# Strided sparse attention feeding a bilinear layer: later batches' attention at other places of the matmul stream, more seven-product pairs, and strided values loaded densely and spread by ScalarE

## The chip, the cores and the metric

The kernel runs on one core of a Trainium2 chip. Its engines work from queues of their own: TensorE (PE, with its weight loads listed as PEld), VectorE (DVE), ScalarE (ACT), GpSimd (POOL) and SyncE (SP); POOL and SP issue nearly all the DMAs. The metric is the device time of one execution in microseconds, lower is better.

## The reference

```python
# q, k, v: (8 batches, 8 heads, 576 positions, 64); scale = 1 / 8
rel = pos[:, None] - pos[None, :]
mask_local = (rel >= 0) & (rel < 32)                       # heads 0 to 3
mask_strided = (rel >= 0) & (pos[None, :] % 32 == pos[:, None] % 32)   # heads 4 to 7
attn = softmax(where(mask, scale * q @ k.T, -1e9))
x = (attn @ v), tokens by heads: 4608 x 512
out = ((x @ w_a) * (x @ w_b)) @ w_out                      # d_ff = 1536
```

## The kernel before

**The bilinear layer sets the pace.** The 4608 tokens are cut into nine tiles t of 512. A tile has 16 slots: twelve feature slots (`ffn_ab`, one block of 128 of the 1536 features each: products with w_a and w_b, 512 columns wide and four deep) and four output slots (`ffn_y` or `ffn_ys`). In this text a slot number counts within its tile, 0 to 11 for features and 12 to 15 for the output stage; tile t's slot s is number 16t + s in the code. An ordinary feature slot puts w_a's product and w_b's product into two PSUM banks; ACT copies the first to `a_sb` (L638) and DVE multiplies the two into `pf` (L641).

**Seven-product pairs.** For some pairs g of feature blocks (2g, 2g+1) the product with w_a is formed from seven half-size products in place of eight (`a_pair_mid` for tiles 3 to 6, listed in `MID_A`; `a_pair` for tiles 7 and 8, listed in `FAST_A`): 14 matmuls of 256 columns in place of 8 of 512. The pair needs four differences of the x tile (`xsum_make`, DVE, L672) and one more bank X: the bank named `e` in `a_pair_mid`. A pair fills slots 2g and 2g+1. From tile 1 on the output stage is done with seven products too (`y_plan`): 14 groups of six matmuls of 256 columns in the order `Y_ORDER`; "yN" is the point just after the Nth group, so y4 lies in slot 13, y7 at its end, y12 in slot 15. It uses sums of `pf` that DVE forms beforehand (`fast_s`, L820); ACT (L851, L857) and DVE (L849, L853, L855) empty its banks.

**Attention is threaded into that stream.** Each later batch b is cut into eight units u, 0 to 3 for the local heads and 4 to 7 for the strided ones. Its steps are:

- D: DMA transposes on SP (`step_D`) that bring k to `kT` and q to `qT`; the rows come from a cast load to DRAM on POOL (`load_qk`);
- Q0 to Q3 (`step_Q`, L338): DVE copies qT into the zero-padded `qz`; Q0 and Q1 are the two halves of the local heads, Q2 and Q3 of the strided heads;
- Su: score matmuls (L381) from `kT` and both halves of `qz` into the one `st` buffer, exp on ACT (L401), mask on DVE (L419);
- Vu for u 0 to 3 (`step_V`): p times `vl` into PSUM bank `o` (L462), then reciprocal (L470) and product (L488) on DVE into `xl`;
- Vu for u 4 to 7 (`step_VT`): p times `vs` into the banks `o` and `e` (L521), Ln twice (L533), Exp (L534) on ACT, two products on DVE (L536) into `xT`;
- O0, O1 (`rows_out`) and I0, I1 (`rows_in`): the local heads' rows go to DRAM and come back transposed into `xT`, both on SP.

The PSUM banks from tile 3 on are three `mm`, one `tp`, the two of `st`, one `o` and one `e`; before tile 3 there is no `e`, and `o` is one buffer of two banks. A buffer that is single is free again when its last reader has ended.

**The order is written out by hand.** `STEPS` (batches 1, 2), `LATER` and `IN_Y` (batches 3 to 7) give for each step the slot after which it is issued; `run` issues all of a step's instructions, on every engine, at that point, and the code keeps each engine's instructions in that order. In `LATER` a number x means slot 16(b-1) + x, so -4 is slot 12 of tile b-2 and 0 is slot 0 of tile b-1; `IN_Y` gives places yN in the output stage of tile b-1. Loads, D, `wsum_make`, `xsum_make` and `fast_s` are placed by `do(slot, ...)`; within a slot the matmuls come first, then the steps of the tables, then the `do` entries. From slot 14 on POOL's work of a slot waits behind a small copy into `pace` of what the slot made.

Of the kernel before, what the change touches and what calls it, by code (L numbers as in the profile page):

```python
# [8 lines left out]
BF16 = mybir.dt.bfloat16  # L9
# [5 lines left out]
FIRST_D = 2  # L15
RL = 6
RS = 8
NP = 72
# [6 lines left out]
VW = 128  # L25
WCH = (0, 2, 5, 9, 12)
FAST_Y = (1, 2, 3, 4, 5, 6, 7, 8)
MID_A = {t: (1, 3) for t in (3, 4, 5, 6)}
FAST_A = {7: (1, 2, 3, 4, 5), 8: (0, 1, 2, 3, 4, 5)}


@with_exitstack
def kernel(
# [10 lines left out]
    nc = tc.nc  # L44
# [23 lines left out]
    def open_psum(stack, **bufs):  # L68
        for nm, n in bufs.items():
# [12 lines left out]
    qT = (const.tile([128, 2, S], BF16, name="qTl"), const.tile([128, HL * W], BF16, name="qTs"))  # L82
    kT_buf = [(const.tile([128, 2, PAD + S], BF16, name=f"kT{i}l"), const.tile([128, 2, RS * GP + 48], BF16, name=f"kT{i}s"))
              for i in range(2)]
    vl_buf = [const.tile([128, HL * 6, VW], BF16, name=f"vl{i}") for i in range(2)]

    p_buf = [const.tile([128, 2, PW], BF16, name=f"p{i}") for i in range(5)]
    vs_buf = [const.tile([NP, HL, RS, VW], BF16, name=f"vs{i}") for i in range(2)]
    mask_l = const.tile([128, 4, LW], I16)
    mask_s = const.tile([NP, NP], I16)  # L90
    nm_l = const.tile([128, 128], BF16, name="nml")
# [139 lines left out]
    def load_vs(b, heads=range(HL)):  # L231
        if b < FIRST_D:

            for z in range(2):
                t = blocks("k", z)
                nc.gpsimd.dma_start(out=t[:NP, :, :RS * D],
                                    in_=v[b, HL + 2 * z:HL + 2 * z + 2].rearrange("h (p r) d -> p h (r d)", r=RS))
                nats[b, "v", z] = t
            return
        for h in heads:  # L240
            nc.gpsimd.dma_start(out=vs_buf[b % 2][:, h, :, 0:D],  # L241
                                in_=v[b, HL + h].rearrange("(p r) d -> p r d", r=RS))

    def spread_vs(b, h, eng):
        eng(vs_buf[b % 2][:, h, :, 0:D], nats[b, "v", h // 2][:NP, h % 2, :RS * D].rearrange("p (r d) -> p r d", r=RS))

    def load_w(c):
        f = slice(128 * WCH[c], 128 * WCH[c + 1])
# [85 lines left out]
    def step_Q(b, z, j):  # L334

        r = slice(64 * j, 64 * j + 64)
        dst = qz_buf[b % 2][j][z][r]
        nc.vector.tensor_copy(dst.rearrange("d c r n -> d (c r n)") if z else dst, qT[z][r])  # L338
# [220 lines left out]
    def step_X(b, c):  # L559
# [15 lines left out]
    STEPS = {1: {5.5: "Tk2", 6: "Tq2", 7: "S4 Tk3", 7.5: "S5", 8: "Tq3", 8.5: "V4", 9: "S6 V5 Pk0", 9.5: "S7 Pq0",  # L575
                 10: "V6 Tk0", 10.5: "Tq0 Pk1", 11: "Pq1", 12: "V7 Tk1 S0 W0 W1", 12.5: "Tq1 W2",
                 12.6: "S1", 12.75: "L0 X2", 13: "s2 X3 V0 m2 L1 W3", 13.5: "V1 S3", 14: "V2 X0", 14.5: "V3", 15: "X1"},
             2: {18: "Q0 Q1", 20: "S0", 20.5: "S1", 21: "V0", 21.5: "S2 Q2", 22: "V1 Q3", 22.5: "S3 O0", 23: "V2", 23.5: "S4",
                 24: "V3 I0 O1", 24.5: "S5", 25.5: "V4", 26: "S6", 26.5: "I1", 27: "V5", 27.5: "S7", 28.5: "V6", 30: "V7"}}
    LATER = {-4: "Q0", -3: "Q1", -1: "S0", 0: "S1", 1: "V0", 2: "S2 Q2", 3: "V1 O0", 4: "S3 I0 Q3", 5: "V2", 6: "S4", 7: "V3 O1", 8: "S5", 9: "V4 I1",  # L580
             10: "S6",
             11: "V5"}
    IN_Y = {2: "S7", 6: "V6", 11: "V7"}
    FN = {"Tk": step_Tk, "Tq": step_Tq, "S": step_S, "V": step_V, "X": step_X, "W": lambda b, n: fast_w(n, slice(0, 3)),
          "s": S_px, "m": S_m, "L": lead_vl, "O": rows_out, "I": rows_in, "Pk": lambda b, c: pair_up("k", c), "Pq": lambda b, c: pair_up("q", c),
          "Q": lambda b, n: step_Q(b, n // 2, n % 2)}

    def run(b, slot):
        for s in slot:
# [13 lines left out]
    def mm_bank(shape):  # L603
        nm = "tp" if used[0] % 4 == 3 and used[0] >= 0 else "mm"
        used[0] += 1
        return psum4[nm].tile(shape, F32, tag=nm, name="mm")
# [61 lines left out]
    def xsum_make(t, n):  # L668
        s_ = xsum[t]
        a, b = ((x_part(t, 0, 1), x_part(t, 0, 0)), (x_part(t, 1, 1), s_[:, 0]), (x_part(t, 1, 1), x_part(t, 0, 1)),  # L670
                (x_part(t, 1, 0), s_[:, 1]))[n]
        nc.vector.tensor_tensor(s_[:, n], a, b, op=ALU.subtract)  # L672
# [3 lines left out]
    def a_pair_mid(t, g):  # L676

        pf = pfs[t]
        X = psum4["e"].tile([128, 512], F32, tag="e", name="e")[:, :HT]
        Y, Z, b1, b0 = [mm_bank([128, TTOK]) for _ in range(4)]  # L680
        Y, Z = Y[:, :HT], Z[:, :HT]
        a = [fsb.tile([128, TTOK], F32, tag="a_sb", name="a_sb", bufs=3) for _ in range(2)][::-1]
        p7 = fsb.tile([128, HT], F32, tag="p7", name="p7")
        quarter = lambda e, k: a[e][:, HT * k:HT * (k + 1)]

        def P(bank, lhs, rhs, start=False):
            for c in range(2):
                nc.tensor.matmul(bank, lhsT=lhs(c), rhs=rhs(c), start=start and c == 0, stop=c == 1, skip_group_check=True)

        w = lambda e, j: (lambda c: wav[:, j, c, g, e])  # L690
        ws = lambda n: (lambda c: wsum_a[n][:, c, g])
        x = lambda j, k: (lambda c: x_part(t, j, k)[:, c])
        xs = lambda n: (lambda c: xsum[t][:, n, c])

        def b_mm(bank, e, kks):
            f = 2 * g + e
            x0 = TTOK * t % (XR * S)
            for kk in kks:
                for k in range(2) if x0 + TTOK > XR * S else (None,):
                    rhs = x_part(t, kk // 2, k)[:, kk % 2] if k is not None else xT[:, kk, x0:x0 + TTOK]  # L700
                    dst = bank if k is None else bank[:, HT * k:HT * (k + 1)]
                    nc.tensor.matmul(dst, lhsT=wb_sb[:, kk, 128 * f:128 * (f + 1)], rhs=rhs,  # L702
                                     start=kk == 0 and k in (None, 0), stop=kk == KD - 1 and k in (None, 1))

        def mult(e, bank):
            halves = lambda v_: v_.rearrange("p (a i s) -> p a i s", i=2, s=16)
            nc.vector.tensor_mul(pf[:, 2 * g + e, :].rearrange("p (i a s) -> p a i s", i=2, s=16), halves(a[e]), halves(bank))

        def add(q, other):
            nc.vector.tensor_tensor(q, other, q, op=ALU.add)  # L710

        P(Y, w(0, 1), x(1, 0), True)
        P(X, w(0, 0), x(0, 0), True)
        nc.scalar.copy(quarter(0, 0), X)
        b_mm(b1, 1, (0, 1, 2))
        P(X, ws(1), xs(1))
        nc.scalar.copy(quarter(1, 0), X)
        P(Z, ws(2), xs(2), True)
        nc.scalar.copy(p7, Z)
        b_mm(b1, 1, (3,))  # L720
        add(quarter(0, 0), Y)
        yield p7[:1, :1]
        P(X, ws(0), xs(0))
        nc.scalar.copy(quarter(1, 1), X)
        b_mm(b0, 0, (0,))
        P(Z, w(1, 1), xs(3))
        add(quarter(1, 0), Z)
        add(quarter(1, 1), p7)
        b_mm(b0, 0, (1, 2, 3))
        P(X, ws(3), x(1, 1))  # L730
        nc.scalar.copy(quarter(0, 1), X)
        mult(1, b1)
        mult(0, b0)
        yield pf[:1, 2 * g, :1]
# [242 lines left out]
    with tc.manual_schedule(engines={ENG.PE, ENG.SP, ENG.Pool, ENG.DVE, ENG.Activation}):  # L977
# [76 lines left out]
        for t in range(NT):  # L1054
            slots += [(ffn_ab, t, f) for f in range(FD)] + [(ffn_ys if t in FAST_Y else ffn_y, t, j) for j in range(4)]
        for b in range(1, B):
            for pos, names in (STEPS.get(b) or {16 * (b - 1) + x: n for x, n in LATER.items()}).items():
                steps.setdefault(pos, []).append((b, names.split()))
            if b not in STEPS:
                for n, names in IN_Y.items():  # L1060
                    steps["y", b - 1, n] = [(b, names.split())]

        at = {}

        def do(i, fn, *args):
            at.setdefault(i, []).append(lambda: fn(*args))
# [10 lines left out]
        for b in range(FIRST_D, B):  # L1077
            g0 = 16 * (b - 2)
            if b == FIRST_D:
                do(0, load_qk, b, False)  # L1080
                do(1, load_qk, b, True)
                do(14, load_vl, b)
                for h in range(HL):
                    do((16, 18, 19, 20)[h], load_vs, b, (h,))
            else:
                do(19 if b == FIRST_D + 1 else g0 - 2, load_qk, b, False)
                do(21 if b == FIRST_D + 1 else g0 + 2, load_qk, b, True)
                for h in range(HL):
                    do(g0 + h + (15 if b == FIRST_D + 1 else 10), load_vs, b, (h,))
                do(g0 + (12 if b == FIRST_D + 1 else 7), load_vl, b)  # L1090
            gs = {2: (13, 14, 15, 15), 3: (6, 6, 14, 15)}.get(b) or (3, 4, 10, 11)
            for (z, nm), g in zip(((0, "k"), (0, "q"), (1, "k"), (1, "q")), gs):
                do(g0 + g, step_D, b, z, nm)
        for n in range(4):
            for c in range(2):
                do(16 * 2 + (2, 5, 7, 9, 11, 13, 14, 15)[2 * n + c], wsum_make, n, c)
        for t in MID_A:
            do(16 * t - 1, xsum_make, t, 0)
            for n in (1, 2, 3):
                do(16 * t, xsum_make, t, n)  # L1100
        do(16 * (NT - 2) - 1, xsum_make, NT - 2, 0)
        for n in (2, 1, 3):
            do(16 * (NT - 2), xsum_make, NT - 2, n)
        for n in range(4):
            do(16 * (NT - 2) + 12 + n, xsum_make, NT - 1, n)
        for h in range(HL):
# [61 lines left out]
```

## Time and profile before

| | before |
|---|---|
| runs, us | 323.25, 323.65, 330.45; median 323.65 |
| profiled execution, us | 323.88, of which the profiled span is 322.2 |
| busy us | PE 313.8, DVE 248.4, ACT 191.4, POOL 120.2 |
| DMA | 40.41 MB in 127811 packets |
| `vs` loads on POOL | 24 of 72 KB, 905 ns each to issue, 4.9 us to landing (median) |
| feature slots of tiles 3, 4, 5 begin at | 126.8, 160.2, 193.7 us |
| output stages of tiles 2, 3, 4, 5 begin at | 116.6, 150.0, 183.5, 216.8 us |

The page gives busy time and counts for each engine. In the order of time, each line has a start, a duration, engine, line, operation, what it writes and reads, the form, how many instructions are merged, and in square brackets the engine's idle time before it and what ended it. Ends of matmuls are modelled, so their durations overlap; their starts are measured. A few per cent of the matmul records are missing.

### The profile page before, as it was taken

What the parts mean: (1) busy time and instruction counts of PE and PEld (TensorE: products, weight loads), DVE (VectorE), ACT (ScalarE), POOL (GpSimd) and SP (SyncE); (2) the same over time, 40 slices, a digit from 0 to 9 for tenths busy, and PEclk for the clock granted to TensorE, in tenths of its full rate; (3) what the DMA queues carried; (4) which work ended last, traced back from release to release, by engine and by line L of the source; (5) the groups of instructions that cost most, each with busy time, mean ns of one, the idle gap of its engine ahead of it and who ended that gap; (6) DMA issues with size and microseconds to landing.
All of it is one profiled execution on the core that took longest, in us unless ns stands there. A gap on an engine that the chain in (4) does not pass through costs nothing. (4 is left out here: it accounts for less than half of the span.)

```text
span 322.2 us, 7287 instructions
## 1 busy us (share of the span) xinstructions
PE 313.8 (97%) x2738; PEld 217.9 (68%) x2766; DVE 248.4 (77%) x569; ACT 191.4 (59%) x371; POOL 120.2 (37%) x211
## 2 busy tenths in 40 slices
PE   8999999999999999999999999999999999999994
PEld 7764555455775578556999996559655866786684
DVE  6665797488867988899689868997799667857862
ACT  6763767355854476557655766577656655535541
POOL 8844850881255344315340435134001003203520
PEclk9999999999999999999999999999999999999999
DMA  8999999999599999999997999999235040004004
GB/s 154 146 203 199 203 190 209 174 146 152 119 126 144 209 148 104 144 157 172 123 120 151 164 108 131 158 203 135 18 85 121 2 127 5 0 4 130 3 0 130
DMA packets 127811, 40.41 MB, mean 125 GB/s; under 512 B 115616, under 2 KB 124896, under 8 KB 127584
## 3 DMA queue, kind: packets, MB, share of 16 engines
q0 software_dynamic: 80400, 19.28, 65.3%
q1 hardware_dynamic: 47232, 20.61, 35.9%
q8 instruction: 21, 0.34, 0.5%
q14 instruction: 14, 0.11, 0.1%
q10 hardware_dynamic: 144, 0.07, 0.1%
HBM read 39.12 MB, written 18.28 MB: 178 GB/s over the span
## 5 line engine op out<-in xcount | busy, mean ns | idle before, releaser
L617 PE MATMUL mm<-xT,wb_sb 128*128 128x512 bf16 (+1 forms) x301 | 71.6, 357 | 0.4
L617 PE MATMUL mm<-xT,wa_sb 128*128 128x512 bf16 (+1 forms) x287 | 70.2, 356 | 0.6
L638 ACT COPY a_sb<-mm 128x512 f32<-128x512 f32 x68 | 39.7, 584 | 29.5 <-PE mm L617 27.8
L1134 POOL CAST pace<-pf 1x1 f32<-1x1 bf16 x68 | 18.5, 273 | 87.6 <-DVE pf L641 41.0
L617 PEld LDWEIGHTS <-wb_sb 128*128 128x128 bf16 x312 | 30.0, 98 | 27.8 <-issue 0.7
L641 DVE TENSOR_TENSOR pf<-a_sb,mm 128x512 bf16<-128x512 f32 x58 | 39.4, 680 | 9.4 <-ACT a_sb L638 5.7
L401 ACT ACTIVATE p<-st 72x576 bf16<-72x576 f32 (+1 forms) x56 | 36.4, 650 | 15.4 <-PE st L381 14.7
L617 PEld LDWEIGHTS <-wa_sb 128*128 128x128 bf16 x312 | 27.9, 98 | 17.8
L886 PEld LDWEIGHTS <-ps 128*128 128x128 bf16 x336 | 32.6, 98 | 4.1 <-issue 0.5
L886 PE MATMUL mm<-wf,ps 128*128 128x256 bf16 x252 | 30.0, 273 | 0.3 <-ACT y_sb L851 0.3
L851 ACT COPY y_sb<-mm 128x512 f32<-128x512 f32 (+1 forms) x32 | 17.9, 558 | 19.1 <-PE mm L886 16.4
L1134 POOL COPY pace<-y_sb 1x1 f32<-1x1 f32 x21 | 8.4, 401 | 51.2 <-DVE y_sb L849 23.6
L886 PEld LDWEIGHTS <-pf 128*128 128x128 bf16 x252 | 23.6, 98 | 2.7
L766 PE MATMUL mm<-xT,wb_sb 128*128 128x512 bf16 x83 | 25.3, 379 | 0.1
L241 POOL DMA_DIRECT2D vs<-in_v_dram x24 | 21.7, 905 | 4.1 <-issue 1.7
L886 PE MATMUL mm<-wo_sb,pf 128*128 128x256 bf16 x168 | 21.8, 273 | 0.0
L820 DVE TENSOR_TENSOR ps<-pf 128x512 bf16<-128x512 bf16 (+1 forms) x49 | 19.6, 399 | 0.8
L702 PE MATMUL mm<-xT,wb_sb 128*128 128x512 bf16 (+1 forms) x80 | 19.1, 337 | 0.0
L419 DVE TENSOR_TENSOR p<-p,mask_l 128x576 int16<-128x576 int16 x32 | 14.5, 452 | 5.6 <-ACT p L401 5.5
L536 DVE TENSOR_TENSOR xT<-o,xr 64x288 bf16<-64x288 f32 x16 | 7.6, 477 | 13.5 <-ACT xr L534 13.4
L462 PEld LDWEIGHTS <-p 128*128 128x128 bf16 (+1 forms) x256 | 12.9, 97 | 7.1 <-DVE xl L488 1.1
L488 DVE TENSOR_TENSOR xl<-o,rc 96x384 bf16<-96x384 f32 x24 | 13.3, 553 | 0.8
(212 smaller groups left out, 644.0 us busy)
## 6 DMA issues: line engine op xcount, KB each, us to landing
out_dram<-y_sb SPq DMA_DIRECT2D x14, 512.0 KB, 4.6
kr<-in_k_dram POOLq DMA_DIRECT2D x12, 288.0 KB, 6.2
qr<-in_q_dram POOLq DMA_DIRECT2D x12, 288.0 KB, 7.1
vl<-in_v_dram POOLq DMA_DIRECT2D x6, 384.0 KB, 9.3
out_dram<-y_sb SPq DMA_DIRECT2D x7, 256.0 KB, 5.5
vs<-in_v_dram POOLq DMA_DIRECT2D x24, 72.0 KB, 4.9
xd<-xl SPq DMA_DIRECT2D x12, 144.0 KB, 3.3
wo_sb<-in_moe_w_out_dram POOLq DMA_DIRECT2D x4, 384.0 KB, 10.7
```

Source lines behind the costliest of these rows:

```text
L241: nc.gpsimd.dma_start(out=vs_buf[b % 2][:, h, :, 0:D], in_=v[b, HL + h].rearrange("(p r) d -> p r d", r=RS))
L401: nc.scalar.activation(p_flat(p)[:M, :2 * W].rearrange("p (i n) -> p i n", n=2 * n), st[:M].rearrange("p a (i n) -> p (a i) n", n=256)[:, ...
L419: nc.vector.tensor_tensor(pi, pi, mk, op=ALU.bitwise_and)
L617: nc.tensor.matmul(ps_[:, c0:c0 + n], lhsT=w[:, kk, 128 * f:128 * (f + 1)], rhs=xT[:, kk, x0:x0 + n], start=(kk == first and c0 == 0), sto ...
L638: nc.scalar.copy(a_sb, ab[0])
L641: nc.vector.tensor_mul(pf[:, f, :].rearrange("p (i a s) -> p a i s", i=2, s=16), halves(a_sb), halves(ab[1]))
L702: nc.tensor.matmul(dst, lhsT=wb_sb[:, kk, 128 * f:128 * (f + 1)], rhs=rhs, start=kk == 0 and k in (None, 0), stop=kk == KD - 1 and k in (N ...
L766: nc.tensor.matmul(got[e], lhsT=wb_sb[:, kk, 128 * f:128 * (f + 1)], rhs=xT[:, kk, x0:x0 + TTOK], start=kk == 0, stop=kk == KD - 1)
L820: nc.vector.tensor_tensor(s[:, n], a, b, op=op)
L851: nc.scalar.copy({"1": part(0, 0), "7": part(0, 1), "6": part(1, 0), "5": part(1, 1)}[k], bank)
L886: nc.tensor.matmul(bank[b][:, q], lhsT=lhs(g, q), rhs=rhs(g), start=k in "172" and q == 0 and g == 0, stop=g == FG - 1, skip_group_check=True)
L1134: nc.gpsimd.tensor_copy(pace, done)
```

## The change

- `LATER` is replaced for batches 4 to 7 and now also holds places in output stages: ("y", N) with positive N is yN of tile b-1, with negative N it is y(14+N) of tile b-2. S0 goes from slot 15 of tile b-2 to y4 of that tile, S1 from slot 0 to y7, S4 from slot 6 to y12, V0 from slot 1 to y13; Q0 and Q1 from slots 12 and 13 to 11 and 12, Q2 and Q3 from slots 2 and 4 of the next tile to 13; in tile b-1, V1 goes from slot 3 to 1, V4 from 9 to 2, V2 from 5 to 3, V3 from 7 to 5, V5 from 11 to 6, V6 from y6 to 10, V7 from y11 to y2. Batch 3 keeps the old places (`THIRD`).
- More seven-product pairs, also at g = 0; there two of the pair's banks are exchanged, and one matmul pair of w_b is issued earlier in every mid pair. The four x differences of tiles 4 to 7 are made at y7 and y9 of the tile before.
- The strided values of a batch come by one load into `v_rows`, and ScalarE copies each head into `vs` (R0 to R3). `vl` rows become 66 elements wide in place of 128. Loads and the transposes of the strided heads are issued some slots sooner.

```diff
-MID_A = {t: (1, 3) for t in (3, 4, 5, 6)}
-FAST_A = {7: (1, 2, 3, 4, 5), 8: (0, 1, 2, 3, 4, 5)}
+MID_A = {3: (2, 4), 4: (0, 2, 4), 5: (0, 2, 4), 6: (0, 2, 4)}
+FAST_A = {7: (0, 1, 2, 3, 4, 5), 8: (0, 1, 2, 3, 4, 5)}
...
-    vl_buf = [const.tile([128, HL * 6, VW], BF16, name=f"vl{i}") for i in range(2)]
+    vl_buf = [const.tile([128, HL * 6, D + 2], BF16, name=f"vl{i}") for i in range(2)]
+    v_rows = const.tile([NP, HL, RS * D], BF16, name="v_rows")
...
-        for h in heads:
-            nc.gpsimd.dma_start(out=vs_buf[b % 2][:, h, :, 0:D],
-                                in_=v[b, HL + h].rearrange("(p r) d -> p r d", r=RS))
+        nc.gpsimd.dma_start(out=v_rows, in_=v[b, HL:].rearrange("h (p r) d -> p h (r d)", r=RS))
...
-        eng(vs_buf[b % 2][:, h, :, 0:D], nats[b, "v", h // 2][:NP, h % 2, :RS * D].rearrange("p (r d) -> p r d", r=RS))
+        src = v_rows[:, h] if b >= FIRST_D else nats[b, "v", h // 2][:NP, h % 2, :RS * D]
+        eng(vs_buf[b % 2][:, h, :, 0:D], src.rearrange("p (r d) -> p r d", r=RS))
...
-    LATER = {-4: "Q0", -3: "Q1", -1: "S0", 0: "S1", 1: "V0", 2: "S2 Q2", 3: "V1 O0", 4: "S3 I0 Q3", 5: "V2", 6: "S4", 7: "V3 O1", 8: "S5", 9: "V4 I1",
-             10: "S6",
-             11: "V5"}
-    IN_Y = {2: "S7", 6: "V6", 11: "V7"}
+    THIRD = {-4: "Q0", -3: "Q1", -1: "S0 R0", 0: "S1", 1: "V0 R1", 2: "S2 Q2", 3: "V1 O0 R2 R3", 4: "S3 I0 Q3", 5: "V2", 6: "S4", 7: "V3 O1", 8: "S5",
+             9: "V4 I1", 10: "S6", 11: "V5", ("y", 2): "S7", ("y", 6): "V6", ("y", 11): "V7"}
+    LATER = {-8: "R0", -7: "R1", -5: "Q0 R2", -4: "Q1 R3", ("y", -10): "S0", ("y", -7): "S1", -3: "Q2 Q3", ("y", -2): "S4", ("y", -1): "V0",
+             0: "S2", 1: "V1 O0", 2: "V4 S3", 3: "V2 S5 I0", 5: "V3 O1", 6: "V5 S6", 7: "I1", 9: "S7", 10: "V6",
+             ("y", 2): "V7", ("y", 7): "x0 x1", ("y", 9): "x2 x3"}
...
+        if g == 0:
+            Z, b1 = b1, Z
...
+        b_mm(b0, 0, (0,))
         P(X, ws(0), xs(0))
         nc.scalar.copy(quarter(1, 1), X)
-        b_mm(b0, 0, (0,))
+        b_mm(b0, 0, (1,))
...
-        b_mm(b0, 0, (1, 2, 3))
+        b_mm(b0, 0, (2, 3))
...
+                if isinstance(pos, tuple):
+                    pos = ("y", b - 1, pos[1]) if pos[1] > 0 else ("y", b - 2, 14 + pos[1])
...
-                for h in range(HL):
-                    do(g0 + h + (15 if b == FIRST_D + 1 else 10), load_vs, b, (h,))
+                do(g0 + (10 if b == FIRST_D + 1 else 4), load_vs, b)
...
-            gs = {2: (13, 14, 15, 15), 3: (6, 6, 14, 15)}.get(b) or (3, 4, 10, 11)
+            gs = {2: (13, 14, 15, 15), 3: (6, 6, 14, 15)}.get(b) or (3, 4, 8, 8)
```

## The prediction, made before the changed kernel ran

> **What bounds the kernel now.** I read the busy row and the slices of the page first, then the stretches tile by tile, then PE, ACT and DVE in order of time around one output stage, then each attention product with the VectorE work that empties its bank, then SP's queue with its landings.
>
> ```profile
> PE 313.8 (97%) x2738; PEld 217.9 (68%) x2766; DVE 248.4 (77%) x569; ACT 191.4 (59%) x371; POOL 120.2 (37%) x211
> PEclk9999999999999999999999999999999999999999
> ```
>
> PE is the bound, at full clock throughout. The order of time on PE shows how dense it is (start, duration, instruction):
>
> ```profile
> 148.92 1.03 PE L617 MATMUL mm<-xT,wb_sb 128*128 128x512 bf16 x4
> 149.78 0.30 PE L521 MATMUL o<-p,vs 72*128 72x72 bf16 x4
> 151.36 0.41 PE L381 MATMUL st<-qz0s,kT0s 128*128 128x144 bf16 x4
> 151.61 2.78 PE L886 MATMUL mm<-wf,ps 128*128 128x256 bf16 x24
> 154.23 0.30 PE L521 MATMUL o<-p,vs 72*128 72x72 bf16 x4
> 154.36 0.29 PE L521 MATMUL e<-p,vs 72*128 72x72 bf16 x4
> 154.49 1.48 PE L886 MATMUL mm<-wf,pf 128*128 128x256 bf16 x12
> ```
>
> Each group's duration holds about 0.17 us of tail that overlaps the next, so starts are the measure. 24 matmuls of 256 columns run from 151.61 to 154.23: 0.109 us each. Four of 512 run from 148.92 to 149.78: 0.216. A strided V takes 0.26 (154.23 to 154.49), an S 0.25, a local V 0.17. After tile 3 has begun PE loses well under 1 us in holes all told. So nothing can be won by filling holes; only fewer columns make it faster, and every new hole is paid in full.
>
> **What the change removes.** Seven-product pairs go from 8+11 to 11+12: four more. An ordinary pair of feature blocks is 16 x 0.216 = 3.46 us for w_a and w_b; a seven-product pair is 14 x 0.109 + 8 x 0.216 = 3.25. Gain 4 x 0.2 = **-0.8 us**. The extra adds and copies of a pair (three DVE adds of 0.41, ACT 5 x 0.37 instead of 2 x 0.58) are off PE.
>
> **What costs nothing, and its cover.** The 24 ScalarE spreads have no row in this shape; the nearest are 0.58 (128x512 copy L638) and 0.37 (128x256), so about 0.58 each, 13.9 us of ACT in all. ACT stands idle 29.5 us before the L638 copies alone, mostly waiting for PE; I take 0, and 13.9 if that cover were gone. POOL loses 24 issues at 0.905 (21.7 us) and gets six; it is 37% busy and only has to be early. The new load starts four slots before its first spread; the old vs loads landed in 4.9 us (median), four slots are about 7. vl rows at a step of 66 elements: old vl loads landed in 9.3 us; tile 3's landed at 154.3, V0's new turn is some 9 us later. Moving the four xsum subtractions (0.42 each) into the output stage lifts DVE there from 7.6 of 10.2 us to about 9.5, still less than the stage.
>
> **Where the move makes holes.** Queues run in program order. With the new table, in the output stage of tile b-2 the order is: y2 with V7 of batch b-1 (its last VectorE work is two products that wait for Ln, Ln, Exp on ScalarE), then at slot 12 Q1 of batch b (a VectorE copy), then y4 with S0 of batch b. S0 reads both halves of qz, so PE must wait for Q1, Q1 stands behind V7's products, and these wait for ScalarE. The old kernel shows that very chain, with V6 at y6 and Q1 behind it, where nobody needed Q1 for another 2 us:
>
> ```profile
> 154.47 0.58 ACT L851 COPY y_sb<-mm 128x512 f32<-128x512 f32 x1 [0.77 <-PE mm L886]
> 155.08 0.43 ACT L533 ACTIVATE xr<-o 64x288 f32<-64x288 f32 x1
> 155.40 0.42 ACT L533 ACTIVATE xr<-e 64x288 f32<-64x288 f32 x1
> 155.85 0.68 ACT L534 ACTIVATE xr<-xr 64x576 f32<-64x576 f32 x1
> ```
> ```profile
> 156.57 0.47 DVE L536 TENSOR_TENSOR xT<-o,xr 64x288 bf16<-64x288 f32 x1 [2.02 <-ACT xr L534]
> 156.95 0.47 DVE L536 TENSOR_TENSOR xT<-e,xr 64x288 bf16<-64x288 f32 x1
> 157.45 0.46 DVE L338 COPY qz1l<-qTl 64x1152 bf16<-64x1152 bf16 x1
> ```
>
> From V6's first matmul (154.23) to Q1's end (157.91) is 3.68 us. In the new order PE has 0.26 (V7) + 12 x 0.109 = 1.57 us of work between V7 and S0. Hole: 3.68 - 1.57 = 2.1 us, in tiles 3, 4 and 5: **+6.3**. Queued behind S0 on PE is the rest of the output stage; nothing refills it.
>
> Tile 2: S7 of batch 3 stands at y2 and V5 before it. In the old trace V5's product ended at 119.86; add Q0 0.45, one weight sum 0.56, S7's mask 0.45, Q1 0.45: 121.8. S0's turn is 118.19 + 1.31 = 119.5. **+2.1** (from 1.5 to 2.8). There V7 of batch 3 (y11) and V0 of batch 4 (y13) also share the one o bank: V7's start to the end of its product was 2.98 us (124.35 to 127.33), the work between is 0.26 + 1.31 + 0.25 = 1.82: 1.2, and DVE has more queued there: **+1.4** (0 to 2).
>
> The second kind of hole is the o bank, of which there is one. That it stops PE when two V's are one slot apart is in the old trace, in batch 2:
>
> ```profile
> 73.49 0.36 PE L462 MATMUL o<-vl,p 128*128 128x65 bf16 x6
> 76.09 0.36 PE L462 MATMUL o<-vl,p 128*128 128x65 bf16 x6 [0.27 <-DVE xl L488]
> ```
>
> V2 begins at 73.49, its normalising product ends at 76.03, V3 begins at 76.09. Old later batches keep V's two slots apart; the new table has V1, V4 at slots 1, 2 and V3, V5 at 5, 6, and in tiles 4 to 6 V1, in tiles 3 to 6 V3, comes at the end of a seven-product pair, behind two multiplies:
>
> ```profile
> 167.69 0.34 PE L462 MATMUL o<-vl,p 128*128 128x65 bf16 x6
> ```
> ```profile
> 168.56 1.28 DVE L707 TENSOR_TENSOR pf<-a_sb,mm 128x512 bf16<-128x512 f32 x2
> 169.76 0.18 DVE L470 RECIPROCAL rc<-o 96x6 f32<-96x6 f32 x1
> 169.98 0.55 DVE L488 TENSOR_TENSOR xl<-o,rc 96x384 bf16<-96x384 f32 x1
> ```
>
> Start to free bank: 2.84 here, of which up to 0.45 is a Q copy that now moves away; I take 2.65. One slot later the next V is due after 0.17 + 8 x 0.216 = 1.89. Hole 0.75 (0.4 to 1.0): three times at V4, four at V5, 0.2 at tile 3's V4: +5.4. Last, V5 at slot 6 holds the e bank until its second product ends, 2.7 to 3.1 us (rows of V4 and V5), and the pair of slot 8 wants e as X after 0.26 + 0.25 + 1.73 + 0.22 = 2.45: 0.4 in four tiles, +1.6 (0.8 to 2.6). Bank holes together **+7.0** (4 to 10).
>
> **The sum** against the profiled execution's own 323.88 us (span 322.2; median of the runs 323.65): -0.8 + 6.3 + 2.1 + 1.4 + 7.0 = +16.0, so about **340 us**. Its own range is 335 to 345.
>
> **Rivals.**
> (1) Only the output-stage holes appear. DVE does less in the feature slots than before (Q2, Q3, three xsums and two masks leave; tile 4 had 20.6 busy of 23.3), so the normalising could come soon enough: 323.9 - 0.8 + 9.8 = 333 us. Against it: the two multiplies and the normalising alone are 2.0 us, more than 1.89. Chance 0.17.
> (2) Not slower: VectorE takes what is ready, so Q1, whose input had landed 5 us earlier or more, passes V7's products at y2. If Q1 ends within 1.57 us of V7's first matmul the large hole is gone, and normalising that passes the multiplies closes the small ones: 323.9 - 0.8 = 323.1 us. Against it: DVE sat 2.02 us before L536 with a landed Q1 behind it, and ran Q1 next. Chance 0.09; it holds also that I misread the place of Q1.
> (3) Late transposes on top. Q2 and Q3 now stand at slot 13, S4 at y12. In the old tile 4 the last qTs landed 40.5 us after the tile's start (37.8 in tile 3); V3 and the loads move up by about 3.4, giving 37.1, and S4's turn is at 23.2 + 2 + 7.85 + 0.75 + 2.1 = 35.9. With the 0.9 of the two copies that is up to 2 us more in three tiles: 345 us. For it: old Q2 once waited 0.5 us for qTs. Chance 0.08.
> (4) The clock falls after the holes. Old PE had a hole of 0.76 us at 42 and kept 9s all through, so rows give no price but bounds: from 0 to the remaining 60 matmuls of an output stage at half rate, 6.5 us in four tiles, 340 to 366; nearest to the row, little. Chance 0.06. [...]
>
> **How the numbers follow.** Forecast 0.60, rivals 0.17, 0.09, 0.08, 0.06. Two per cent, about what a measurement of this kernel can tell from no change, is 6.5 us: slower begins at 330.1. Rival 2 and a 0.02 tail of rival 1 lie within it: same 0.11. Faster would need 6.5 us where 0.8 are to be had: 0.01. Slower 0.88. The range 331 to 346 leaves out rival 2 and the upper parts of 3 and 4.
>
> **What would show it.** Right: PE holes of about 2 us before L381 after y4 in four output stages, ended by DVE L338; holes of 0.5 to 1 before L521 in tiles 3 to 6, ended by DVE xl; before the X product of slot 8, ended by DVE xT; output stages of tiles 2 to 5 about 2 us or more longer than tile 6's. ACT busy near 207, POOL near 105. Wrong: Q1 ending before S0's turn, or V4 and V5 starting with no idle before them; then the time stays near 323.

## The result: 345.6 us against 324.4, and the profile after

| | before | changed |
|---|---|---|
| runs of this comparison, us | 323.25, 323.65, 325.17, 330.45; median 324.41 | 342.71, 343.68, 347.58, 348.83; median 345.63 |
| ratio, 95% interval | | 1.0637 (1.0499 to 1.0775) |
| profiled execution, us (span) | 323.88 (322.2) | 342.71 (341.0) |
| busy us | PE 313.8, DVE 248.4, ACT 191.4, POOL 120.2 | PE 319.0, DVE 252.9, ACT 204.6, POOL 105.0 |

Ratios here and below leave out single disturbed executions (above the one of 348.83), so they can lie a little below the quotient of the medians. The forecast was 340.0, the range 331 to 346; the median lies 0.4 us below the upper end. The busy row, the DMA row (mean busy share of the 16 DMA engines in each of the 40 slices) and the clock row of the changed kernel's page:

```profile
PE 319.0 (94%) x2751; PEld 219.1 (64%) x2782; DVE 252.9 (74%) x580; ACT 204.6 (60%) x407; POOL 105.0 (31%) x180
PEclk9999999999999979999999999999999999999999
DMA  9999999997998966999099935999016012004004
```

PE's share falls from 97% to 94%, and one slice has a 7 in the clock row, where the kernel before had 9s only. ACT (207 forecast) and POOL (105 forecast) came out as worked out.

**The chain behind V7.** PE in order of time in tile 3's output stage (start, duration, instruction; in brackets the idle time before it and what ended it):

```profile
158.40 0.29 PE L521 MATMUL o<-p,vs 72*128 72x72 bf16 x4
158.54 0.29 PE L521 MATMUL e<-p,vs 72*128 72x72 bf16 x4
158.66 1.48 PE L890 MATMUL mm<-wf,ps 128*128 128x256 bf16 x12
162.10 0.41 PE L381 MATMUL st<-qz1l,kT1l 128*128 128x192 bf16 x3 [1.96 <-DVE qz1l L338]
```

V7 starts at 158.40, the two groups of six take until 159.97 (158.66 + 12 x 0.109), and S0 starts at 162.10: a hole of 2.13. What S0 waits for, first on ACT, then on DVE, in the same stage:

```profile
159.26 0.43 ACT L533 ACTIVATE xr<-o 64x288 f32<-64x288 f32 x1
159.58 0.41 ACT L533 ACTIVATE xr<-e 64x288 f32<-64x288 f32 x1
160.03 0.68 ACT L534 ACTIVATE xr<-xr 64x576 f32<-64x576 f32 x1
```
```profile
160.74 0.47 DVE L536 TENSOR_TENSOR xT<-o,xr 64x288 bf16<-64x288 f32 x1 [0.80 <-ACT xr L534]
161.12 0.46 DVE L536 TENSOR_TENSOR xT<-e,xr 64x288 bf16<-64x288 f32 x1
161.59 0.46 DVE L338 COPY qz1l<-qTl 64x1152 bf16<-64x1152 bf16 x1
```

Q1 (161.59) stands behind V7's two products, and these behind Ln, Ln, Exp, as forecast.

**The one o bank.** PE and then DVE around slots 5 and 6 of tile 4:

```profile
181.77 0.35 PE L462 MATMUL o<-vl,p 128*128 128x65 bf16 x6
...
184.21 0.30 PE L521 MATMUL o<-p,vs 72*128 72x72 bf16 x4 [0.35 <-DVE xl L488]
```
```profile
182.18 1.28 DVE L710 TENSOR_TENSOR pf<-a_sb,mm 128x512 bf16<-128x512 f32 x2
183.38 0.18 DVE L470 RECIPROCAL rc<-o 96x6 f32<-96x6 f32 x1
183.60 0.55 DVE L488 TENSOR_TENSOR xl<-o,rc 96x384 bf16<-96x384 f32 x1
```

V5 starts 2.44 us after V3, 0.51 later than the matmuls between them allow, and it is the product into `xl`, behind the pair's two multiplies, that frees the bank (183.60 + 0.55 = 184.15).

**What the sum did not hold.** PE in tile 2's output stage:

```profile
118.25 1.47 PE L890 MATMUL mm<-wf,ps 128*128 128x256 bf16 x12
121.87 0.41 PE L381 MATMUL st<-qz0l,kT0l 128*128 128x192 bf16 x3 [2.15 <-DVE qz0l L338]
122.12 2.12 PE L890 MATMUL mm<-wf,ps 128*128 128x256 bf16 x12
```

Twelve matmuls of 256 columns have a duration of 1.47 before the hole and 2.12 after it: from 122.78 to 126.19, 3.41 us, PE ran at half rate (0.214 instead of 0.109 us from start to start), which costs half of that, 1.7 us.

In tile 3 ACT and then PE show a second wait that the sum did not hold. R0, the first spread of a batch, waits for the dense load; the copy `a_sb` stands behind it, and PE waits for the copy:

```profile
151.98 0.62 ACT L245 COPY vs<-v_rows 72x512 bf16<-72x512 bf16 x1 [0.62 <-DMA v_rows<-in_v_dram]
152.50 0.36 ACT L728 COPY a_sb<-e 128x256 f32<-128x256 f32 x1
```
```profile
152.91 0.38 PE L691 MATMUL e<-xT,tq 128*128 128x256 bf16 x2 [0.51 <-ACT a_sb L728]
```

The holes of the profiled execution, each the time from one matmul's start to the next beyond the usual distance of that shape:

| what | forecast us | measured us |
|---|---|---|
| S0 behind Q1, tiles 3, 4, 5 | 6.3 | 2.13 + 2.14 + 2.14 = 6.4 |
| S0 in tile 2 | 2.1 | 2.31 |
| V0 in tile 2, o bank | 1.4 | 0.85 |
| o and e banks in tiles 3 to 6 | 7.0 | 6.3: V4 1.8, V5 2.1, V2 0.6, X products 1.8 |
| half rate after the tile 2 hole | in a rival only | 1.7 |
| S4 waiting for qTs (205.47) | in a rival only | 0.7 |
| a_sb behind R0, which waits for `v_rows` (152.91) | 0 | 0.7 |

These come to 18.9; less the forecast 0.8 of the pairs 18.1, where the span grew by 18.8.

### The profile page after: what moved, and what is told of

It is laid out like the page before. It is cut to its first block, busy times and chain, and to the rows that moved or that the text cites. A ratio compares the mean times of both kernels' runs of the same rounds, so it can differ in the third digit from the quotient of the medians.

```text
span 341.0 us, 7304 instructions
## 1 busy us (share of the span) xinstructions
PE 319.0 (94%) x2751; PEld 219.1 (64%) x2782; DVE 252.9 (74%) x580; ACT 204.6 (60%) x407; POOL 105.0 (31%) x180
## 4 chain that ended last, share of the span: by engine, by line
PE 73%; DVE 11%; ACT 7%; DMA 4%; issue 3%; SPq 1%; DVEq 0%; ACTq 0%; POOL 0%; POOLq 0%
PE mm L618 22%; PE mm L890 14%; PE mm L770 5%; PE st L381 3%; PE mm L705 3%; PE ax L763 3%; PE mm L952 3%; PE misc L158 3%; PE mm L763 2%; DMA v_rows<-in_v_dram 2%; DVE pf L710 2%; PE e L691 2%; PE o L462 2%; PE mm L917 2%; PE o L521 1%
## 5 line engine op out<-in xcount | busy, mean ns | idle before, releaser
L618 PE MATMUL mm<-xT,wb_sb 128*128 128x512 bf16 (+1 forms) x258 | 61.7, 359 | 0.4
L618 PE MATMUL mm<-xT,wa_sb 128*128 128x512 bf16 (+1 forms) x250 | 60.7, 358 | 0.6
L1133 POOL CAST pace<-pf 1x1 f32<-1x1 bf16 x57 | 17.2, 301 | 104.2 <-DVE pf L642 53.0
L639 ACT COPY a_sb<-mm 128x512 f32<-128x512 f32 x60 | 35.0, 583 | 21.8 <-PE mm L618 20.0
L618 PEld LDWEIGHTS <-wb_sb 128*128 128x128 bf16 x272 | 26.0, 98 | 25.0 <-issue 0.6
L642 DVE TENSOR_TENSOR pf<-a_sb,mm 128x512 bf16<-128x512 f32 x50 | 34.0, 679 | 6.5 <-ACT a_sb L639 4.3
L618 PEld LDWEIGHTS <-wa_sb 128*128 128x128 bf16 x272 | 24.0, 97 | 16.0
L770 PE MATMUL mm<-xT,wb_sb 128*128 128x512 bf16 x90 | 27.4, 379 | 0.1
L705 PE MATMUL mm<-xT,wb_sb 128*128 128x512 bf16 (+1 forms) x110 | 26.3, 332 | 0.0
L1133 POOL COPY pace<-y_sb 1x1 f32<-1x1 f32 x17 | 5.4, 319 | 66.6 <-DVE y_sb L853 40.5
L536 DVE TENSOR_TENSOR xT<-o,xr 64x288 bf16<-64x288 f32 x16 | 7.6, 478 | 13.7 <-ACT xr L534 13.7
L245 ACT COPY vs<-v_rows 72x512 bf16<-72x512 bf16 x24 | 14.6, 614 | 0.6 <-DMA v_rows<-in_v_dram 0.6
L710 DVE TENSOR_TENSOR pf<-a_sb,mm 128x512 bf16<-128x512 f32 x22 | 14.1, 684 | 0.4
```

The lines of the kernel that those rows point to most:

```text
L618: nc.tensor.matmul(ps_[:, c0:c0 + n], lhsT=w[:, kk, 128 * f:128 * (f + 1)], rhs=xT[:, kk, x0:x0 + n], start=(kk == first and c0 == 0), sto ...
L639: nc.scalar.copy(a_sb, ab[0])
L642: nc.vector.tensor_mul(pf[:, f, :].rearrange("p (i a s) -> p a i s", i=2, s=16), halves(a_sb), halves(ab[1]))
L770: nc.tensor.matmul(got[e], lhsT=wb_sb[:, kk, 128 * f:128 * (f + 1)], rhs=xT[:, kk, x0:x0 + TTOK], start=kk == 0, stop=kk == KD - 1)
L1133: nc.gpsimd.tensor_copy(pace, done)
```

## The experiments

Each group ran on one chip beside the kernel before, whose medians were 323.14, 323.28, 323.41 and 323.65 in the four groups.

| kernel | median us | ratio to before (95%) |
|---|---|---|
| after_again | 343.51 | 1.0618 (1.0563 to 1.0673) |
| q_first | 340.03 | 1.0520 (1.0472 to 1.0568) |
| v_mid | 343.35 | 1.0616 (1.0561 to 1.0671) |
| filler | 340.95 | 1.0529 (1.0480 to 1.0578) |
| both | 335.56 | 1.0321 (1.0247 to 1.0395) |
| both_v | 334.67 | 1.0313 (1.0258 to 1.0368) |
| dense_only | 323.88 | 1.0007 (0.9979 to 1.0036) |
| fixed | 339.84 (runs 334.89 to 341.56) | not given |
| late_r | 338.09 | 1.0440 (1.0378 to 1.0503) |
| late_fix | 339.63 | 1.0483 (1.0434 to 1.0533) |
| strided | 348.13 | 1.0757 (1.0701 to 1.0813) |
| both_strided | 343.92 | 1.0602 (1.0537 to 1.0667) |

**after_again**: the changed kernel once more, as the base of the first group.

> The changed kernel unaltered, beside the three below. Theory A (Q1 behind V7 and the single o and e banks make the holes; the clock falls to half for 3.4 us after some of the 2.1 to 2.3 us holes, and how often depends on the execution): 341 to 349 us, the four S0 holes at 2.1 to 2.3 us each in every execution, and a slower execution shows more half-clock stretches. Rival B (the spread from 342.7 to 348.8 comes from other stalls, such as DMAs that land at other times): a slower execution shows other or longer holes and the same clock.

343.51 us, the S0 holes again 2.31, 2.13, 2.13 and 2.13. Two stretches of half rate here, of 3.41 us each, against one in the execution of 342.71; the four executions (341.74 to 345.27) had granted clocks of 0.995 to 0.987, the longest the lowest. That is theory A, but the other holes moved too: V0 in tile 2 waited 1.57 us in place of 0.85, and `a_sb` did not wait for R0.

**q_first**: takes away the wait of S0, by putting Q0 and Q1 ahead of V7.

```diff
-    LATER = {-8: "R0", -7: "R1", -5: "Q0 R2", -4: "Q1 R3", ...
+    LATER = {-8: "R0", -7: "R1", -6: "Q0 Q1", -5: "R2", -4: "R3", ...
```

> Q0 and Q1 of batches 4 to 7 both move to slot 10, ahead of V7's products; all else as in the changed kernel. Theory A: S0 no longer waits, the four holes (2.31, 2.13, 2.14, 2.14 = 8.7 us) and the half-clock stretches (1.8 to 5 us) go, the bank holes (7.0 us) stay: 331 to 334 us, full clock throughout. Rival B (S0 waits for something else that is late at y4 too, the transposes or ScalarE, and Q1 is only the last to be seen): the holes shrink by less than half, 337 us or more. Rival C (VectorE is simply overloaded in the output stage): the time lost moves to y8 to y14 or to the next tile's start, 337 us or more.

340.03 us; theory A's 331 to 334 was missed. The S0 holes went (0.41 left in tile 2, none in tiles 3 to 5), but 8.7 us of holes gave only 3.5. Tile 4's output stage shows one that came in their place, on PE and then on DVE:

```profile
202.06 0.51 PE L381 MATMUL st<-qz0s,kT0s 128*128 128x144 bf16 x4 [2.10 <-DVE qz0s L338]
202.37 1.48 PE L890 MATMUL mm<-wo_sb,ps 128*128 128x256 bf16 x6
```
```profile
200.99 0.92 DVE L338 COPY qz0s<-qTs 64x1152 bf16<-64x1152 bf16 x2 [3.13 <-DMA qTs<-qr]
```

S4 now waits 2.27 us, because Q2 and Q3 wait 3.13 for the transposed queries; in the changed kernel the same S4 came behind an S0 hole of 2.14 and waited 0.68. One stretch of half rate, 3.41 us from 202.23 on, follows the S4 hole. Holes of 1.26 and 0.63 at slot 9 (behind ACT's wait for `v_rows`), V0 in tile 2 at 2.04 in place of 0.85, and 0.35 in each of three output stages took more. That the S0 chain is as I described it was shown; that its removal is worth its length was not.

**v_mid**: takes away the neighbouring V's: V1 goes to slot 0, V3 to slot 4.

```diff
-             0: "S2", 1: "V1 O0", 2: "V4 S3", 3: "V2 S5 I0", 5: "V3 O1", 6: "V5 S6", ...
+             0: "V1 O0 S2", 2: "V4 S3", 3: "V2 S5 I0", 4: "V3 O1", 6: "V5 S6", ...
```

> V1 moves from slot 1 to 0 and V3 from 5 to 4 in batches 4 to 7, into the middle of a pair, so that o has two slots to come free before V4 and V5; all else as in the changed kernel. Theory A: the holes at V4 (0.13, 0.40, 0.65, 0.65) and V5 (0.51 to 0.54, four times) go, 4.0 us; the S0 holes, the clock and the holes before the pair's X product (0.26) stay: 4 us below the changed kernel of the same job. Rival C (VectorE has too much in the feature slots, so any normalising comes late): less than 1.5 us gained, the holes turn up at V2, V6 or at the multiplies' banks.

343.35 us, level with the changed kernel, so theory A was missed; of rival C the size came true, not its cause. The holes before V4 and V5 (3.9 us) went, and holes of 1.99, 2.04 and 1.81 came at the pair of slot 8. ACT and then PE in tile 3:

```profile
152.26 0.62 ACT L245 COPY vs<-v_rows 72x512 bf16<-72x512 bf16 x1 [1.94 <-DMA v_rows<-in_v_dram]
152.78 0.36 ACT L728 COPY a_sb<-e 128x256 f32<-128x256 f32 x1
```
```profile
153.20 0.38 PE L691 MATMUL e<-xT,tq 128*128 128x256 bf16 x2 [1.82 <-ACT a_sb L728]
```

R0 waits for the dense load, the pair's copy `a_sb` stands behind R0 in ACT's queue, PE waits for the copy. O1's store was now issued 0.7 to 1.3 us after the load (5.3 to 7.3 in the changed kernel), and the load took longer to land, a median of 7.9 us and at most 9.0, against 6.5 and 8.1. That the store is what made the load late is likely, but was not tested.

**filler**: leaves every wait, but PE does 20 matmuls more ahead of S0, into a quarter of S0's buffer that S0 does not use.

```diff
+            if b > FIRST_D + 1 and u == 0:
+                for _ in range(20):
+                    nc.tensor.matmul(sv[:, 3, :192], lhsT=kT[:, 0, :128], rhs=kT[:, 0, :192], start=True, stop=True)
```

> Twenty 192-column matmuls into an unused quarter of the st buffer are put ahead of S0 of batches 4 to 7 (1.6 us of PE work inside holes of 2.1 us); all else as in the changed kernel, and the output is the same. Theory A with the clock falling because PE stands idle: the order of everything else and S0's start stay, no half-clock stretch is left, 340.5 to 342 us with little spread. Rival D (the clock falls for another reason, load or temperature): half-clock stretches as in the changed kernel. Rival E (the holes are not idle waits, PE's queue being short of instructions): the added matmuls cost their 6.6 us on top, 347 us or more.

340.95 us. The three executions from 340.01 to 341.11 had a granted clock of 0.997 to 0.998, and the profiled one, 341.11, has no stretch of half rate; the fourth took 350.30 at 0.994 and was not traced. PE at the same place of tile 2:

```profile
118.74 1.47 PE L893 MATMUL mm<-wf,ps 128*128 128x256 bf16 x12
120.23 1.81 PE L371 MATMUL st<-kT0l 128*128 128x192 bf16 x20
122.49 0.41 PE L384 MATMUL st<-qz0l,kT0l 128*128 128x192 bf16 x3 [0.45 <-DVE qz0l L338]
122.74 1.47 PE L893 MATMUL mm<-wf,ps 128*128 128x256 bf16 x12
```

S0 starts no sooner, 3.75 us after the group before it (3.62 without the filler), and the 12 matmuls behind it run at full rate. So idle PE is what lowers the clock here, and the loss of clock is worth about 343.5 - 340.9 = 2.6 us in the median. By the three shorter executions rivals D and E fell.

**both**: q_first and v_mid together.

> q_first and v_mid together: Q0 and Q1 are issued at slot 10 of the tile before, V1 at slot 0, V3 at slot 4. Theory A (two independent kinds of TensorE hole, the S0 ones and the bank ones, and the load of the dense values as a third limit that appears when either is removed): the S0 holes (8.7 us in the changed kernel) and the V4/V5 holes (4 us) are both gone from the trace, but the waits of ScalarE for v_rows and of DVE for the transposed queries stay or grow, so the time falls by less than the sum: 336 to 341 us, with holes ended by the ScalarE copy a_sb at slot 9's pair of 1 to 2 us in each of three tiles. Rival B (the gains of q_first were eaten by the bank holes and not by the landings, and those of v_mid by the S0 holes): together they give the whole 12.7 us, 329 to 332 us, and ScalarE's waits for v_rows are below 1 us in all.

335.56 us (331.90 to 339.14), between the two expectations. Alone the edits were worth 3.5 and 0.2 us, together 8.0. Each alone had met a wait that is shorter with both: the S4 holes of q_first (2.27 in tile 4) are 0.1 at most, and the slot 9 holes of v_mid (5.8 in sum) are 3.1. Why these landings fit better with both was not tested. The profiled execution, 331.90 us, has no half-rate stretch; against the kernel before it keeps holes of 2.04 in tile 2 (V0), 1.53, 0.94 and 0.62 at slot 9 (ACT waits 2.9 us for `v_rows`) and about 0.35 in three output stages:

```profile
128.59 0.34 PE L462 MATMUL o<-vl,p 128*128 128x65 bf16 x6 [1.88 <-DVE xT L530]
```

V0 of batch 4 waits for the o bank, which V7 of batch 3 holds until its product has run, and that stands in DVE's queue behind sums of the output and of the weights.

**both_v**: both, with the dense load at slot 1 instead of 4. Here and in fixed the load for batch 4 overtakes the spreads of batch 3, so two strided heads of batch 3 get batch 4's values. The work is the same, but R2 and R3 of batch 3 now wait for the load of batch 4 in tile 2: ACT 3.4 us here and 3.0 in fixed, PE 0.9 and 0.5.

```diff
-                do(g0 + (10 if b == FIRST_D + 1 else 4), load_vs, b)
+                do(g0 + (10 if b == FIRST_D + 1 else 1), load_vs, b)
```

> both, and the dense load of the values issued at slot 1 of the tile instead of slot 4 (three slots, about 4 us sooner). Theory A (ScalarE's spread R1 waits for a landing that comes too late, and the pair's copy a_sb stands behind it): ScalarE's waits for v_rows go from about 5 us to under 1 us in all, the holes at slot 9's pair go with them, and the time falls 3 to 5 us below that of both: 332 to 336 us. Rival B (the landing is limited by what shares the DMA rings at that point, and moves along with the issue only in part; or the sooner load delays the store and transposes of the output instead): the time stays within 1.5 us of both's, and new waits stand at the transposes of the queries.

334.67 us, level with both, as in rival B. The profiled execution was the longest of the four (347.10 against 332.93 to 335.80). In it the holes at slot 9 of tiles 3 to 5 are gone, and holes of 1.9, 3.0, 2.2 and 5.1 stand before S0 or S4, all behind `qTl` or `qTs`. Whether these waits also grew in the three shorter executions is not known.

**dense_only**: only the dense load, the spreads and the narrower `vl`, with the old order and the old pairs (load at slot 10, spreads at the places of `THIRD`).

> The kernel before, with the one part of the change that replaces the strided loads of the values: one dense load for each batch, four copies on ScalarE, the local values' tile with a step of 66; the order of the attention steps, the pairs and the sums of the inputs stay as before. Theory A (the prediction: ScalarE's copies, 24 of about 0.61 us or 14.6 us in all, lie in its slack and cost nothing; GpSimd is not on the path): 322 to 325 us, ratio 0.997 to 1.006. Rival B (the copies stand in ScalarE's queue ahead of a_sb and exp, each one delays TensorE by part of its 0.6 us): up to 4 us slower, 326 to 328 us, with holes ended by ScalarE at the slots where R stands.

Ratio 1.0007 (0.9979 to 1.0036): theory A. The spreads as a group of the profile by line (engine, form, count, busy us, mean ns, idle before them):

```profile
L245 ACT COPY vs<-v_rows 72x512 bf16<-72x512 bf16 x24 | 14.3, 617 | 0.0
```

14.3 us more on ACT, no wait for the load, nothing on the time. So the loss needs the rest of the change: the new order with its pairs, its sooner loads and transposes, and the x differences in the output stage. These were not all taken apart.

**fixed**: both_v, the strided transposes of the second half at slot 6 instead of 8, R2 and R3 one slot sooner, and for batch 4 V0 after the output stage.

```diff
-            gs = ... or (3, 4, 8, 8)
+            gs = ... or (3, 4, 6, 6)
-    LATER = {..., -6: "Q0 Q1", -5: "R2", -4: "R3", ...
+    LATER = {..., -6: "Q0 Q1 R2", -5: "R3", ...
+    FOURTH = {**LATER, ("y", -1): "", 0: "V0 S2", 1: "V1 O0"}
```

> both_v, and three more moves: the query and key transposes of the second half of the heads are issued at slot 6 instead of 8 (ahead of the output's own transposes), the last two spreads stand at slots 10 and 11 instead of 11 and 12, and in the one tile where the attention of the batch before ends late (batch 4's start, tile 2) V0 comes after the output stage. Theory A (each remaining hole is a wait that comes from the place in a queue, and all can be placed away): all S0, V0, S4 and slot-9 holes below 0.5 us, no stretch at half clock, 322 to 327 us, so about level with the kernel before. Rival B (the work of half an output stage more in flight needs more of DVE and of the rings at one point than there is, and holes only move): 330 us or more, with the sum of the holes unchanged from both_v within 2 us and standing at other instructions.

339.84 us, so theory A was missed. V0's hole in tile 2 went and so did those at slot 9, but in tile 5 Q0 and Q1 waited 3.45 us for `qTl`, with a hole of 2.2 before S0: SP issued that transpose only at 221.74, behind the issue of `kT1l` that took from 210.99 to 218.19 and two stores, and it landed at 230.01. S4 of tile 3 waited 1.3 and V4 0.7. The granted clock of the four executions was 0.982 to 0.992. Not all of the distance to both is the edit's: in the profiled execution the output stage of tile 1, ahead of every moved step, begins at 86.5 in place of 81.9, with a hole of 2.52 at 41.87 and half rate from 42.44 on. So fixed shows that holes moved to other instructions, which is rival B, but not whether it is slower than both_v.

**late_r**: the other way round from both_v: load at slot 10, spreads only where a product is about to read them.

```diff
-    LATER = {-8: "R0", -7: "R1", -6: "Q0 Q1", -5: "R2", -4: "R3", ..., ("y", -1): "V0",
-             ... 3: "V2 S5 I0", 4: "V3 O1", 6: "V5 S6", 7: "I1", ...
+    LATER = {-6: "Q0 Q1", ..., ("y", -1): "V0 R0",
+             ... 3: "V2 S5 I0 R1", 4: "V3 O1", 6: "V5 S6 R2", 7: "I1 R3", ...
-                do(g0 + (10 if b == FIRST_D + 1 else 4), load_vs, b)
+                do(g0 + 10, load_vs, b)
```

> The kernel both, with the dense load of the values and ScalarE's spreads put late instead of soon: the load at slot 10 as in the kernel before (in both: slot 4), the four spreads at the end of the output stage and at slots 3, 6 and 7 of the next tile (in both: slots 8, 9, 11, 12 of the tile before), each still ahead of the first product that reads its head (slots 2, 6, 10 and the output stage). Theory A (in both, the spreads stand in ScalarE's queue ahead of a_sb and wait for a landing that the crowded rings bring late, for no need): the holes at slot 9's pair (1.53, 0.94 and 0.62 us in both) and those of 0.35 us in the output stages go, nothing takes their place, 327 to 331 us. Rival B (what is moved away from slot 4 collides at slot 10 with the four transposes of the strided queries, as the sooner load collided with those of the first half): S4 waits for the transposed queries by 1 to 3 us in each of two or three tiles, 332 to 336 us.

338.09 us, no faster than both; theory A was wrong. Rival B had the place right, but it was one tile and one larger wait, not two or three of 1 to 3. ACT no longer waits for `v_rows`, but the spreads at slots 3, 6 and 7 stand ahead of the pairs' copies (holes of 0.56 to 0.70, two in each of tiles 3 to 6), and the load at slot 10 meets the strided transposes. DVE and then PE in tile 2:

```profile
128.74 0.92 DVE L338 COPY qz0s<-qTs 64x1152 bf16<-64x1152 bf16 x2 [4.07 <-DMA qTs<-qr]
```
```profile
129.81 0.64 PE L381 MATMUL st<-qz0s,kT0s 128*128 128x144 bf16 x4 [3.65 <-DVE qz0s L338]
```

A hole of 3.8 us, and 6.83 us of half rate from 129.01 on.

**late_fix**: late_r and, for batch 4, V0 after the output stage.

```diff
+    FOURTH = {**LATER, ("y", -1): "R0", 0: "V0 S2", 1: "V1 O0"}
```

> late_r, and in the one tile in which the batch before ends late (tile 2), V0 of the next batch comes after the output stage instead of in it. Theory A (that V0 waits 2.04 us for the o bank, which the last product of the batch before holds): the hole of 2.0 us in tile 2 goes, holes of 0.3 to 0.7 us come at slots 0 to 3 of tile 3, where V1 and V4 follow one slot closer: 1 to 2 us below late_r, 325 to 329 us, still not below the kernel before. Rival B (the bank is held just as long, and the wait moves to V1 and V4 whole): level with late_r within 0.7 us, with holes of 2 us in sum in the first four slots of tile 3.

339.63 us, 1.5 above late_r where 1 to 2 below was expected; the two intervals overlap by more than half, so the two may be level. V0's hole in tile 2 (1.23 us, in a stretch of half rate) went; holes before S4 in tiles 3 and 5 (0.5 and 0.3) and 0.64 before V4 came, and S4 in tile 2 stayed at 3.9. Neither theory fits, and what makes up the difference is open.

**strided** and **both_strided**: the changed kernel and both, each with four strided loads at slots 8 to 11 and no spreads.

```diff
-        nc.gpsimd.dma_start(out=v_rows, in_=v[b, HL:].rearrange("h (p r) d -> p h (r d)", r=RS))
+        for h in heads:
+            nc.gpsimd.dma_start(out=vs_buf[b % 2][:, h, :, 0:D],
+                                in_=v[b, HL + h].rearrange("(p r) d -> p r d", r=RS))
...
-                do(g0 + (10 if b == FIRST_D + 1 else 4), load_vs, b)
+                for h in range(HL):
+                    do(g0 + h + (15 if b == FIRST_D + 1 else 8), load_vs, b, (h,))
```

> The changed kernel with its new order and pairs, but the values of batches 2 and later come as before, by four strided loads (at slots 8 to 11 of the tile) and without the spreads on ScalarE. Theory A (the loss is the order's: Q1 behind V7 and the single o bank; the dense load costs nothing where the S0 and bank holes are): the S0 holes of 2.1 to 2.3 us and the bank holes stay where they are, the one hole at slot 9 that waited for the dense values (0.67 us) goes, 341 to 345 us, ratio to the kernel before 1.054 to 1.067. Rival B (the dense load and the 24 spreads on ScalarE are a real part of the loss in this order: ScalarE's spreads stand ahead of V7's Ln and Exp and of a_sb): 333 to 339 us, with S0 holes below 1.7 us.

> The kernel both with the values by four strided loads (slots 8 to 11) and without the spreads. Theory A (in both, what is left of the loss is ScalarE's wait for the dense values at slot 9, 3.1 us in sum, the V0 hole of 2.0 us in tile 2, and halves of the clock): the holes at slot 9 go and nothing replaces them, 328 to 333 us. Rival B (the rings are too full in the second half of a tile whatever form the values come in; late_r showed it with one dense load at slot 10): the transposes of the strided queries land late, S4 waits 2 to 4 us in at least one tile and the clock halves behind it, 335 to 340 us.

348.13 and 343.92 us: 4.6 and 8.4 above the same order with the dense load. Theory A of both missed (341 to 345 and 328 to 333), and so did rival B of the first (333 to 339); the S0 holes stayed at 2.13 to 2.32, as its theory A had them. Rival B of the second had the place right and the size too small. The transposed strided queries of both and then of both_strided, by tile (what DVE sat idle for, us and times; time from issue to landing):

```profile
  DMA qTs<-qr: 0.7, 2
...
DMA to landing us min/median/max: 2.7/5.0/6.7
```
```profile
  DMA qTs<-qr: 15.2, 4
...
DMA to landing us min/median/max: 4.8/7.9/9.9
```

The slot 9 holes of both are gone, but four holes of 5.2, 2.6, 1.9 and 2.9 us before S4 and 13.7 us at half rate outweigh them. So the dense load, worth nothing in the old order, is worth much in the new one. The strided loads stand at other slots than the dense one, so form and place change together; late_r, with the dense load at slot 10, lies between both and both_strided (338.09).

## Why the prediction was right, and which terms were not

**The bound** held: PE is full, every new hole is paid. Holes and clock make up 18.9 us of a span that grew by 18.8 + 0.8.

**The number** is in part luck. The four S0 holes and the bank holes came out as summed, but three things that the sum put at nothing (the clock, R0 and S4) added 1.7 + 0.7 + 0.7. The profiled execution is 2.7 above the 340.0, and the median, 345.63, lies 0.6 above the forecast's own range of 335 to 345; the stated range, which reaches to 346, holds it. The repeat, after_again, had a median of 343.51.

**S0 behind Q1 behind V7**, +6.3 and +2.1: measured 6.4 and 2.31, with the engines, the lines and the order named in the prediction. q_first took the holes away by moving Q0 and Q1 alone. Rival 2 (VectorE takes what is ready) fell: Q1 ran right behind L536 in tiles 3, 4 and 5, and in tile 2 behind V5's product, a weight sum and S7's mask, as forecast.

**V0 in tile 2**, +1.4: 0.85 here, 1.57 in after_again, 2.04 in q_first. The bank is held by V7's own chain, whose last product stands behind other DVE work, so the hole probably depends on how much delay PE already has had; that was not tested. 0 to 2 was nearly a fair pair of ends.

**The bank holes**, +7.0: 6.3, so rival 1 (none of them) fell. The split was off: V4 0.13 to 0.65 and V5 0.51 to 0.54 where I had 0.75 (0.2 for tile 3's V4); holes of 0.1 to 0.3 before V2 and of 0.24 at the pair with g = 0 that I had not listed made up for it, which is luck. The step at fault is the 2.65 us from start to free bank: V3 to the end of `xl` was 2.38 (181.77 to 184.15). I had taken off only part of the 0.45 of the Q copy; 2.84 less the whole of it is 2.39.

**What was put at nothing.** The spreads and the dense load cost nothing by themselves (dense_only). But I named ACT's idle time as their cover and did not look at what stands behind R0 in ACT's queue (the expectation of both_v calls it R1): when the load lands late, `a_sb` and with it PE wait. I had set four slots, about 7 us, against the 4.9 in which the old loads landed; the dense load took a median of 6.5 and at most 8.1. That cost 0.7 us in the changed kernel and 5.8 in v_mid. A spread that stands ahead of its need is a place where a late landing stops ACT.

**Late transposes** (rival 3, "2 us in three tiles"): one hole of 0.7. The S0 holes ahead of them gave the transposes 2 us more each time. With these gone, waits came in q_first (2.27) and in both_strided (12.6 in sum), but in both, where they are gone too, S4 waits 0.1 us at most. So the rival named the right resource, and the forecast's own holes hid it in part; whether it shows depends also on when the transposes are issued and what lands beside them.

**The clock** (rival 4, chance 0.06): this is 1.7 of the 2.7 us by which the profiled execution lies above 340, and about 2.6 us in the median of after_again by filler. The forecast put nothing on it. The one hole that the rival had a row for, 0.76 us with 9s all through, gave no price for longer ones: here half rate came behind a hole of 2.31, and filler, with PE idle for 0.45 us at that place and the 12 matmuls behind it at 1.47 us in place of 2.12, shows that the idle PE was the cause.

**The pairs**, -0.8, were not measured alone, and no run had the new order with the old pairs. No version with the new order came below the kernel before, and the old order with the dense load is level with it. The DMA row of the kernel before, to set beside that of the changed one, suggests why moves within the new order gave so little:

```profile
DMA  8999999999599999999997999999235040004004
```

Before, the lowest of the first 28 slices is 5 (6 in dense_only); after, there are slices at 0 and 3 among the 9s: the same 40.4 MB come in tighter bursts. Where a transfer was moved within them, a later landing went with it: the dense load of v_mid (a median of 7.9 us in place of 6.5), the transposed strided queries of late_r (5.9, against 5.0 in both) and of both_strided (7.9). What sets a single landing, the engines' fullness or the order in one queue, was not shown apart.

## What to carry to other kernels

When a step is moved forward in a hand-written order, write down for each of its operands which copy, transpose and load makes it, and what each of these stands behind in its queue: here a copy that nobody had waited for became the path through the work in front of it. The gain from removing a stall is limited by the next landing that the stall covered: of 8.7 us of S0 holes all but 0.41 went in q_first, and the time fell by 3.5. Gains do not add up: two fixes were worth 3.5 and 0.2 us alone and 8.0 together. A load's form and place that is neutral in one order may be worth 8 us in another. A hole on a full TensorE may cost more than its length, by the clock that falls behind it: 1.7 us more behind the hole of 2.31.

## What the runs showed of the hardware that was not expected

**The clock fell to half with some of the holes.** In the changed kernel the granted clock is 0.50 from 122.78 to 126.19 us, and 1.00 from 118.00 to 122.78 and from 126.19 to 128.00. Between the start and the end of an execution, every stretch of half rate in these profiles lasted 3.41 or 6.83 us. Three of them, with the hole each came with: 3.41 us with a hole of 2.31 in the changed kernel and of 2.27 in q_first, 6.83 with one of 3.8 in late_r. The stretch began 0.9 us after the hole had ended in the changed kernel (122.78, S0 at 121.87), 0.2 after in q_first (202.23, S4 at 202.06), and 0.8 before the end in late_r (129.01, S4 at 129.81).

The length of a hole alone does not tell whether such a stretch follows: in the profiled execution of the changed kernel one came with the S0 holes of 2.31, 2.13, 2.14 and 2.14, in that of after_again two with those of 2.31, 2.13, 2.13 and 2.13, so behind some of 2.13 and not behind others. In both, with a hole of 2.04 in tile 2, there was none. What decides it was not shown. It is one reason why the time differs between executions of one kernel: the four of after_again run from 341.74 us at a granted clock of 0.995 to 345.27 at 0.987.
